# Tiles of every sixteenth token: dilated attention with V as plain rows, ungated w2 and new queue orders

## The chip, the cores and the metric

The kernel runs on one core of a Trainium2 chip. The core has five engines with a queue each: TensorE (PE, with its weight loads as PEld), VectorE (DVE), ScalarE (ACT), GpSimd (POOL) and SyncE (SP), which here issues nearly all DMAs. Each queue is worked through in order, and semaphores tie the queues together. The metric is the device time of one execution in microseconds; lower is better.

## The reference

One transformer block on x of 2048 tokens by 512, with a modulation from c. Attention has 32 heads of 16 and looks, from token s, at the eight tokens s, s - 2, ..., s - 14; tokens before the start are masked.

```python
mod = (_silu(c) @ w_mod).reshape(c.shape[0], 6, 1, -1)      # sa, ca, ga, sb, cb, gb
h = _layernorm(x) * (1 + ca) + sa
x = x + ga * attention(h, A_wqkv, A_wo)                      # W, dil = 8, 2
h = _layernorm(x) * (1 + cb) + sb
x = x + gb * (silu(h @ B_w1) * (h @ B_w3)) @ B_w2            # 512 -> 1792 -> 512
```

## The kernel before

The 2048 tokens are 16 tiles (T) of 128 partitions. Before the change a tile is 128 consecutive tokens, and x, held in SBUF as `x_sb`, is both the input and the running sum.

**Stages.** Modulation: c goes through a tanh on ScalarE (L465), one VectorE operation (L467), a small transpose on TensorE (L470) and a copy by VectorE (L472); then small products with `wm_s` give scale and shift (L504, L487), products with `wm_g` give the gates (L531, L541). LN1 (`ln_stats`): VectorE takes statistics (L555, L556), GpSimd raises to the power -0.5 (L565), VectorE normalizes (L576, and L571 for tile 0). `ln_T` transposes by TensorE (L636, evictions L644 and L651) or by DMA (L621 scales in place) into `h`. Projections Q and K (L691) and V (L711) follow; ScalarE evicts them (L700, L701, L721). V of a tile is stored to a scratch in DRAM.

**Attention of a tile.** VectorE multiplies q with eight shifted copies of K in one operation (`prod`, L742): 8 x 4 x 128 elements a partition. K lies along the free dimension with a pad of 16 columns in front, so a shift by 2w tokens is a start 2w columns earlier. TensorE sums over the head dimension (`red`, L752); for tile 0 a matmul with `before` (L749) adds the mask. Softmax takes VectorE (L764, L769, L794 to L797) and ScalarE (L782); the weights are transposed (L807, L811). `values` loads V back: partition (token, w) of a block holds the rows that this token sees with this w, four DMAs of 128 overlapping runs of 2 KB (two neighbouring rows each). VectorE weights them (L827, in place in `vsh`), TensorE sums over w (L855), ScalarE evicts (L861), a DMA transposes (`ot`), TensorE multiplies with `wo` (L867; its gate `ga` has been multiplied into `wo`, L946), and VectorE adds to `x_sb` and sums the row (L871).

**FFN.** LN2 (`ln_sums`: L586 to L601) runs on GpSimd and ScalarE. For a group of 2 or 4 tiles (`FFN`) and each of 14 blocks of F, `ffn_unit` makes gate and up (L883), the silu on ScalarE (L889) and the product on VectorE (L892). `ffn_w2` sums over F (L921, and L909 in halves for tiles 14 and 15); the gate `gb` has been multiplied into `w2` (L952, four operations), so VectorE only adds `x_sb` (L931) and the result is stored.

**Order.** The program makes a list of 1118 operations. `ORDER` is a written-out list of their numbers that fixes each engine's queue; `SLOTS` gives each rotating buffer. `Program.synchronize` puts a wait where one is needed. `warm` (L518) makes 24 matmuls on a constant, ahead of the first real work.

## Time and profile before

| What | us |
|---|---|
| runs | 238.07, 239.04, 243.02; median 239.04 |
| span of the profiled execution | 237.7 |
| TensorE busy in it | 229.7 |
| VectorE busy | 179.4 |
| ScalarE busy | 138.5 |
| GpSimd busy | 29.2 |

How full the engines are in 40 slices of 5.9 us (each digit is tenths), with the share of the DMA engines:

```profile
PE   7999999999999998999999999999999999999995
...
DVE  5699999999999989999999999682654403434433
ACT  2289577999978744985865594837473405040300
...
DMA  6999999999999999897981693642203000000202
```

VectorE and the DMA engines are full from slice 3 to about slice 25, while attention runs; after that TensorE works through what is left of the FFN. "Busy" of TensorE counts a matmul from its start to the end of its pipeline, so matmuls overlap in it.

### The profile page before, as it was taken

How to read it: one execution, taken by the hardware profiler on the slowest of the kernel's cores; microseconds unless marked ns; L12 is line 12 of the kernel's file. 1: busy time of each engine (PE TensorE's matmuls, PEld its weight loads, DVE VectorE, ACT ScalarE, POOL GpSimd, SP SyncE). 2: the span in 40 equal slices, each digit the busy share in tenths (PEclk: the TensorE clock that was granted, in tenths of full speed). 3: DMA queues.
4: the chain of work that ended last, by engine and by line, in shares of the span. 5: the costliest groups of instructions: out<-in, count | busy, mean ns of one | idle time of the engine just before them, and what ended most of it. 6: DMA issues, size and time to landing. Idle time of an engine off the chain costs nothing.

```text
span 237.7 us, 4535 instructions
## 1 busy us (share of the span) xinstructions
PE 229.7 (97%) x1781; PEld 136.2 (57%) x1806; DVE 179.4 (75%) x279; ACT 138.5 (58%) x267; POOL 29.2 (12%) x66
## 2 busy tenths in 40 slices
PE   7999999999999998999999999999999999999995
PEld 4776454445588674664444444444475457485774
DVE  5699999999999989999999999682654403434433
ACT  2289577999978744985865594837473405040300
POOL 4434100013002000240002520012010000000000
PEclk9999999999999999999999999999999999999999
DMA  6999999999999999897981693642203000000202
GB/s 216 372 337 322 158 237 299 208 269 283 353 200 270 243 249 199 173 260 177 247 234 47 182 234 72 154 132 46 67 19 91 3 0 0 6 19 0 70 0 88
DMA packets 46317, 38.85 MB, mean 163 GB/s; under 512 B 21704, under 2 KB 37080, under 8 KB 46296
## 3 DMA queue, kind: packets, MB, share of 16 engines
q1 hardware_dynamic: 46288, 38.56, 66.9%
q8 instruction: 14, 0.23, 0.4%
q14 instruction: 7, 0.06, 0.1%
q10 hardware_dynamic: 8, 0.00, 0.0%
HBM read 29.62 MB, written 4.21 MB: 142 GB/s over the span
## 4 chain that ended last, share of the span: by engine, by line
PE 74%; DMA 8%; DVE 8%; SPq 4%; ACT 3%; issue 2%; ACTq 0%; DVEq 0%
PE pall L883 38%; PE pall L921 18%; DMA sb_x<-in_A_x_dram 5%; PE pall L867 5%; SPq L124 4%; PE pall L691 4%; DMA sb_vsh<-v_scratch_dram 3%; PE pall L909 3%; PE pall L855 2%; PE pall L752 2%; PE pall L711 2%; DVE sb_vsh L827 2%; DVE sb_pq L742 2%; DVE sb_hh L892 1%; ACT sb_h L621 1%
## 5 line engine op out<-in xcount | busy, mean ns | idle before, releaser
L883 PE MATMUL pall<-sb_h,sb_w 128*128 128x256 bf16 (+1 forms) x664 | 101.9, 307 | 1.8 <-DVE sb_hh L892 0.9
L883 PEld LDWEIGHTS pall<-sb_h,sb_w 128*128 128x128 bf16 x672 | 64.8, 98 | 37.2 <-issue 2.8
L889 ACT ACTIVATE sb_sg<-pall 128x256 bf16<-128x256 f32 (+1 forms) x84 | 35.6, 453 | 54.1 <-PE pall L883 53.0
L892 DVE TENSOR_TENSOR sb_hh<-sb_sg,pall 128x256 bf16<-128x256 bf16 (+1 forms) x84 | 39.9, 505 | 34.8 <-PE pall L883 32.7
L921 PE MATMUL pall<-sb_w,sb_hh 128*128 128x512 bf16 x190 | 44.0, 379 | 0.3
L742 DVE TENSOR_TENSOR sb_pq<-sb_q,sb_kT 128x4096 bf16<-128x4096 bf16 x16 | 36.3, 2282 | 0.0
L921 PEld LDWEIGHTS pall<-sb_w,sb_hh 128*128 128x128 bf16 x196 | 19.0, 98 | 21.6 <-DVE sb_hh L892 0.4
L691 PE MATMUL pall<-sb_h,sb_wqkv 128*128 128x512 bf16 (+1 forms) x154 | 30.2, 335 | 0.5 <-issue 0.2
L827 DVE TENSOR_TENSOR sb_vsh<-sb_vsh,sb_al 128x4096 bf16<-128x4096 bf16 x12 | 27.3, 2287 | 2.1 <-DMA sb_vsh<-v_scratch_dram 2.1
L621 ACT ACTIVATE sb_h<-sb_h,sb_modc 128x512 bf16<-128x512 bf16 (+1 forms) x24 | 16.5, 743 | 10.1 <-DMA sb_h<-sb_xn 10.1
L691 PEld LDWEIGHTS pall<-sb_h,sb_wqkv 128*128 128x128 bf16 x160 | 14.7, 98 | 11.8 <-ACT sb_ac L861 0.4
L931 DVE TENSOR_TENSOR sb_o<-pall,sb_x 128x512 bf16<-128x512 f32 (+1 forms) x18 | 11.1, 625 | 10.5 <-PE pall L921 6.8
L711 PE MATMUL pall<-sb_wqkv,sb_h 128*128 128x512 bf16 x62 | 15.5, 379 | 0.2
L867 PE MATMUL pall<-sb_wo,sb_ot 128*128 128x512 bf16 x61 | 15.3, 379 | 0.3 <-issue 0.2
L586 POOL TENSOR_SCALAR sb_nm<-sb_sx 128x2 f32<-128x2 f32 x8 | 1.7, 218 | 105.2 <-DVE sb_x L871 105.1
L644 ACT ACTIVATE sb_h<-pall,sb_modc 128x256 bf16<-128x256 bf16 (+1 forms) x18 | 9.9, 612 | 7.5 <-DVE sb_modc L509 6.5
L861 ACT ACTIVATE sb_ac<-pall 128x512 bf16<-128x512 f32 x16 | 9.5, 595 | 7.2 <-PE pall L855 7.1
L601 ACT ACTIVATE sb_xn<-sb_x,sb_nb,sb_rs 128x512 bf16<-128x512 bf16 x16 | 12.4, 806 | 0.7 <-POOL sb_nb L599 0.6
L871 DVE SCALAR_TENSOR_TENSOR sb_x<-pall,sb_x 128x512 bf16<-128x512 f32 x16 | 10.9, 686 | 1.5 <-PE pall L867 1.3
L590 ACT ACTIVATE sb_xn<-sb_x,sb_nm 128x512 bf16<-128x512 bf16 x16 | 11.4, 714 | 0.7 <-POOL sb_nm L586 0.7
L721 ACT ACTIVATE sb_v<-pall 128x512 bf16<-128x512 f32 x16 | 9.5, 600 | 2.8 <-PE pall L711 2.8
L555 DVE BATCH_NORM_STATS2 sb_st<-sb_x 128x6 f32<-128x512 bf16 x16 | 10.6, 680 | 0.8 <-DMA sb_x<-in_A_x_dram 0.7
(87 smaller groups left out, 208.3 us busy)
## 6 DMA issues: line engine op xcount, KB each, us to landing
sb_vsh<-v_scratch_dram SPq DMA_DIRECT2D x48, 256.0 KB, 5.5
sb_vshx<-v_scratch_dram SPq DMA_DIRECT2D x16, 256.0 KB, 4.6
sb_w<-in_B_w_dram SPq DMA_DIRECT2D x6, 512.0 KB, 7.9
sb_w<-in_B_w_dram SPq DMA_DIRECT2D x6, 384.0 KB, 5.4
v_scratch_dram<-sb_v SPq DMA_DIRECT2D x16, 128.0 KB, 6.4
out_dram<-sb_o SPq DMA_DIRECT2D x14, 128.0 KB, 1.8
sb_wqkv<-in_A_wqkv_dram SPq DMA_DIRECT2D x6, 256.0 KB, 6.3
sb_x<-in_A_x_dram SPq DMA_DIRECT2D x4, 256.0 KB, 6.4
```

The costliest lines, as they stand in the source:

```text
L590: p.op("act", lambda e, vn=vn, T=T: e.activation(vn.at[:], x_sb[:, T, :], ACT.Square, bias=nm[:, T, :], accum_out=var[:, T, :]), c_act(512 ...
L601: p.op("act", lambda e, vn=vn, T=T: e.activation(vn.at[:], x_sb[:, T, :], ACT.Identity, bias=nb[:, T, :], scale=rs[:, NT + T, :]), c_act(5 ...
L621: return e.activation(vh.at[:, ft, 0:n * P], vh.at[:, ft, 0:n * P], ACT.Identity, bias=modc[:, 8 * which + ft:8 * which + ft + 1], scale=m ...
L691: ins = e.matmul(bank(vp)[:, j * n:(j + 1) * n], wqkv[:, t, col:col + P], vh.at[:, t, 0:n], start=(t == ORDER[0] and j == 0), stop=(t == O ...
L711: ins = e.matmul(bank(vp), vh.at[:, t, tt * P:(tt + 1) * P], wqkv[:, t, 2 * D:3 * D], start=(t == ORDER[0]), stop=(t == ORDER[-1]))
L742: return e.tensor_tensor(vp.at[:], in0, in1, ALU.mult)
L827: return e.tensor_tensor(v_w, v_w, a_w, ALU.mult)
L867: ins = e.matmul(bank(vy), vt.at[:, ft, :], wo[:, ft, :], start=(ft == 0), stop=(ft == KT - 1))
L883: ins = e.matmul(bank(vp)[:, 0:n], wt[:, t, fi * P:(fi + 1) * P], vh.at[:, t, 0:n], start=(t == 0), stop=(t == KT - 1))
L889: p.op("act", lambda e: e.activation(vt.at[:, 0:n], bank(vgp)[:, 0:n], ACT.Silu), c_act(n), k, r=[vgp], w=[vt], table="silu")
L892: p.op("dve", lambda e: e.tensor_tensor(vh_.at[:, 0:n], vt.at[:, 0:n], bank(vup)[:, 0:n], ALU.mult), c_dve(n), k, r=[vt, vup], w=[vh_])
L921: ins = e.matmul(bank(vz), vhh[fi].at[:, tt * P:(tt + 1) * P], w2[:, fi, :], start=(fi == 0), stop=(fi == NF - 1))
```

## The change

**Tokens.** Partition p of tile T holds token 16 p + res(T), where res(T) = 2 (T mod 8) + T // 8. So tiles 0 to 7 hold the even tokens and 8 to 15 the odd ones, and the token two earlier lies in the tile one below, on the same partition; below the lowest tile of a half it is the highest tile, one partition earlier. K needs no pad and `kT` is 2048 columns.

**Products.** `prod` becomes two operations: w = 0 to u (u = T mod 8) with the tiles T to T - u, on all 128 columns, and the other 7 - u with the tiles from the top of the half, on columns 1 to 127. Column 0 of the second part is preset to a large negative number where a buffer needs it, and this takes the place of the `before` mask. A product now needs K of all eight tiles of its half.

**V.** A store writes rows 16 apart. A load is two DMAs of 512 single rows (1 KB), each row of the half once, and waits for the stores of all eight tiles of the half.

**Gate.** `w2` stays as it is. For tiles 0 to 11 ScalarE evicts the sum, VectorE multiplies with `gb` and adds `x_sb`. Ahead of FFN group [12, 13] two VectorE operations put a gated copy of `w2` into the two `vsh` buffers, for tiles 12 to 15.

**LN1.** The first two tiles are normalized as a pair, like the others; the special case for tile 0 goes. The first two pairs, not only the first, have their projections split by quarter of the contraction (`pieces`).

**Orders.** `ORDER` and `SLOTS` are new throughout (1121 operations). Read back into names, the queues begin and run so:

| Queue | before | after |
|---|---|---|
| SP | x 0-1, wms0, wqk0, x 2-3, wqk1, wqk2, wqk3, wv0, wv1, x 4-5, ... | x 2-3, x 0-1, wms0, wqk0, wv0, x 6-7, wqk1, wv1, x 4-5, x 12-15, wqk2, wqk3, ... |
| PE | 7 warm-ups, transpose of c, 17 warm-ups, transposes of tile 0, two of L504, transposes of tile 1, two of L504, K and Q of tiles 0-1 | 18 warm-ups, transpose of c, 4 warm-ups, transposes of tiles 3 and 2, four of L504, Q and K of tiles 2-3, ... (two warm-ups at the very end) |
| VectorE | c, statistics of tile 0, of tile 1, normalize 0, 1 | c, statistics of tiles 2, 3, then 1, 0, normalize 3, 2, ... |
| VectorE, first product | before the statistics of tile 12 and the last four normalizations | after all statistics and normalizations |
| Attention | tiles 0 to 15, by pairs | pairs 0 to 6, then 10, 8, 12 and 14 |
| SP, first V load | after the stores of V of tiles 0 to 2 | after the stores of V of tiles 0 to 7 |

```diff
-    x_view = x2d.rearrange("(t p) d -> p t d", p=P)
+    NU = NT // 2
+    x_view = x2d.rearrange("(p u e) d -> p e u d", p=P, e=2)
+    out_view = out2d.rearrange("(p u e) d -> p e u d", p=P, e=2)
+
+    def res(T):
+        return 2 * (T % NU) + T // NU
...
-    kT = sb([P, KT, PAD + S], bf, "kT")
+    kT = sb([P, KT, S], bf, "kT")
...
-        vh.pieces = [Val(f"h_{ft}") for ft in range(KT)] if not which and not gi else None
+        vh.pieces = [Val(f"h_{ft}") for ft in range(KT)] if not which and gi < 2 else None
...
-        p.dma(v_dram[PAD + T * P:PAD + (T + 1) * P, :], lambda: vt.at[:], k, (128, 1024), r=[vt], w=[vd], cost=400, store=True)
+        p.dma(bass.AP(v_dram, (PAD + res(T)) * D, [[NT * D, P], [1, D]]), lambda: vt.at[:], k, (128, 1024), r=[vt], w=[vd], cost=400, store=True)
...
-                in0 = bass.AP(vq[cch].at, tt * P, [[KT * 512, P], [0, W], [512, KT], [1, P]])
-                in1 = bass.AP(kT, PAD + T * P, [[KT * (PAD + S), P], [-DIL, W], [PAD + S, KT], [1, P]])
-                return e.tensor_tensor(vp.at[:], in0, in1, ALU.mult)
...
+                row, n = W * KT * P, W - 1 - u
+                q = lambda m, c: bass.AP(vq[cch].at, tt * P + c, [[KT * 512, P], [0, m], [512, KT], [1, P - c]])
+                k = lambda t, m, c: bass.AP(kT, t * P, [[KT * S, P], [-P, m], [S, KT], [1, P - c]])
+                o = lambda w, m, c: bass.AP(vp.at, w * KT * P + c, [[row, P], [KT * P, m], [P, KT], [1, P - c]])
+                if preset.get(vp.slot, W) > u + 1:
+                    e.memset(bass.AP(vp.at, (u + 1) * KT * P, [[row, P], [P, n * KT], [1, 1]]), BEFORE)
+                preset[vp.slot] = u + 1
+                ins = e.tensor_tensor(o(0, u + 1, 0), q(u + 1, 0), k(T, u + 1, 0), ALU.mult)
+                if n:
+                    ins = e.tensor_tensor(o(u + 1, n, 1), q(n, 1), k(top, n, 1), ALU.mult)
+                return ins
...
-        for q in range(4):
-            p.dma(lambda q=q: vv.at[:, 2 * q:2 * q + 2, :],
-                  bass.AP(v_dram, (PAD + T * P + 32 * q) * D, [[2 * D, 16], [-DIL * D, W], [1, 2 * D]]), ("vl", T), (128, 2048),
-                  r=[vv_dram[T]] + ([vv_dram[T - 1]] if T else [vvpad]), part=[vv], group=loads, cost=640, again=True)
+        c = T // NU * NU
+        for b in range(0, 8, 4):
+            p.dma(lambda b=b: vv.at[:, b:b + 4, :],
+                  bass.AP(v_dram, (PAD + res(T) - DIL * (W - 1) + 256 * b) * D, [[2 * D, P], [256 * D, 4], [1, D]]), ("vl", T), (512, 1024),
+                  r=[vv_dram[t] for t in range(c, c + NU)] + [vvpad], part=[vv], group=loads, cost=470)
...
+        vo = Val("o", opool)
+        k = ("zo", T)
+        p.op("act", lambda e: e.activation(vo.at[:], bank(vz), ACT.Copy), c_act(512), k, r=[vz], w=[vo])
+        o = p.op("dve", lambda e: e.tensor_tensor(vo.at[:], vo.at[:], gb_bc[:], ALU.mult), 340, k, r=[vg[1]], w=[vo], lock=True)
+        p.op("dve", lambda e: e.tensor_tensor(vo.at[:], vo.at[:], x_sb[:, T, :], ALU.add), 340, k, r=[vx[T]], w=[vo], lead=o, lock=True)
...
-        vns = [v for pr in ([[T] for T in Ts] if gi == 0 else pairs(Ts)) for v in ln_stats(pr)]
+        vns = [v for pr in pairs(Ts) for v in ln_stats(pr)]
...
+        if Ts[-1] == NT - 3:
+            for i, (a, b) in enumerate(((0, 8), (8, NF))):
+                p.op("dve", lambda e, i=i, a=a, b=b: e.tensor_tensor(w2v[i].at[:, 0:b - a, :], w2[:, a:b, :],
+                                                                     bass.AP(gb_bc, 0, [[D, P], [0, b - a], [1, D]]), ALU.mult),
+                     48 + 274 * (b - a), ("mod", 7 + i), r=vw2 + [vg[1]], w=[w2v[i]], lock=True)
```

105 lines of the change are left out of this document (38 added, 67 removed), and 132 rows, old and new, of tables (ORDER, SLOTS).

## The prediction

> **What bounds the kernel now.** I read the page first: how full each engine is, then the chain of work that ended last.
>
> ```profile
> span 237.7 us, 4535 instructions
> ...
> PE 229.7 (97%) x1781; PEld 136.2 (57%) x1806; DVE 179.4 (75%) x279; ACT 138.5 (58%) x267; POOL 29.2 (12%) x66
> ...
> PE 74%; DMA 8%; DVE 8%; SPq 4%; ACT 3%; issue 2%; ACTq 0%; DVEq 0%
> ```
>
> TensorE is busy for 97% of the span and makes 74% of the chain. Busy can hide gaps, so the next question is pace. Two lines of the chain in order of time (start, length, what) give it:
>
> ```profile
> 188.98 6.04 PE pall L921 x28
> ...
> 207.82 6.11 PE pall L883 x56
> ```
>
> That is 6.04 / 28 = 216 ns for a matmul of 512 columns and 6.11 / 56 = 109 ns for one of 256: a steady stream. Where is TensorE not streaming? The busy time in windows (window, length, PE, weight loads, DVE, ACT, POOL, clock, DMA share, GB/s), and then the timeline of TensorE (start, length):
>
> ```profile
> 10.00:235.00 225.00, 221.62 (x1704) 130.46 (x1727) 172.17 (x252) 136.34 (x264) 24.76 (x46) 1.00 0.67 160
> ```
> ```profile
> 1.24 1.68 PE L518 MATMUL pall<-sb_ones 128*128 128x256 bf16 x7 [1.24 <-DVE sb_ones L375]
> 3.35 0.18 PE L470 MATMUL pall<-sb_ident,sb_c4s 4*128 4x4 bf16 x1 [0.43 <-DVE sb_c4s L467]
> 3.46 3.14 PE L518 MATMUL pall<-sb_ones 128*128 128x256 bf16 x17
> 6.53 0.40 PE L636 MATMUL pall<-sb_ident,sb_xn 128*128 128x128 bf16 x4
> ...
> 7.63 0.54 PE L504 MATMUL pall<-sb_csT_bf,sb_wm_s 128*128 128x1 bf16 x16
> 8.19 0.61 PE L691 MATMUL pall<-sb_h,sb_wqkv 128*128 128x256 bf16 x4
> ...
> 229.73 5.29 PE L909 MATMUL pall<-sb_w,sb_hh 128*128 128x256 bf16 x47
> ```
>
> The projections start at 8.19, the last matmul ends at 235.02, and between 10 and 235 TensorE idles 225.00 - 221.62 = 3.4 us in all. So the span is 8.19 (head) + 223.4 (streaming) + 3.4 (waits) + 2.7 (last result to the end) = 237.7 us. The change keeps every large matmul, so the 223.4 stays. It can win at most the 3.4, and it can lose in the head and in new waits. The profiled span is 1.3 us under the median of the runs, 239.04; I add that 1.3 at the end.
>
> **The head.** In the new queue of TensorE the transpose of c (L470) stands behind eighteen warm-ups; before it stood behind seven. Seven took 1.68 us, the last of them 0.38, so one starts every (1.68 - 0.38) / 6 = 0.217 us: 18 x 0.217 = 3.9, and the transpose starts at 1.24 + 3.9 = 5.15 in place of 3.35. On VectorE the copy of its result stands ahead of the first LN statistics, in both orders:
>
> ```profile
> 3.57 0.16 DVE L472 TENSOR_SCALAR sb_csT_bf<-pall 128x4 bf16<-128x4 bf16 x1 [0.27 <-PE pall L470]
> 3.71 0.69 DVE L555 BATCH_NORM_STATS2 sb_st<-sb_x 128x6 f32<-128x512 bf16 x1
> ...
> 5.73 0.74 DVE L571 SCALAR_TENSOR_TENSOR sb_xn<-sb_x,sb_mv,sb_rs 128x512 bf16<-128x512 bf16 x1
> 6.93 0.41 DVE L576 TENSOR_SCALAR sb_xn<-sb_x,sb_mv,sb_rs 128x512 bf16<-128x512 bf16 x1 [0.46 <-POOL sb_rs L565]
> ...
> 8.43 1.27 DVE L555 BATCH_NORM_STATS2 sb_st<-sb_x 128x6 f32<-128x512 bf16 x2
> ...
> 11.02 0.74 DVE L576 TENSOR_SCALAR sb_xn<-sb_x,sb_mv,sb_rs 128x512 bf16<-128x512 bf16 x2 [1.05 <-POOL sb_rs L565]
> ```
>
> So the statistics move from 3.71 to 3.71 + 1.8 = 5.5. A pair then goes as the pair at 8.43 did: 11.02 - 8.43 = 2.6 to the first normalized tile and 0.74 for two, so 8.85; the other pair's two statistics fill the 1.05 us wait. From the last normalized tile to the first projection it was 8.19 - 7.34 = 0.85; all 32 small products of L504 now lie in that stretch and not 16 of them, which adds about 0.25. Start: 9.95, **+1.75 us**. The joint pair saves nothing that shows: L571 at 0.74 becomes a 0.41, inside this sum. Swapping loads (x of tiles 2 and 3 first, `wms0` third) moves `wms0` back by one issue and 256 KB, but its use moves from 6.76 to 9.1. Lower bound +1.0, if the warm-ups ran at the pace of the seventeen, (3.14 - 0.38) / 16 = 0.173.
>
> **Attention waits for eight tiles.** Keys and V rows of one tile now come from all eight tiles of its half. The first product, which began at 22.89 with keys of four tiles, needs 10.4 us of projections for four tiles (2 x 32 x 0.109 + 2 x 8 x 0.216 for each two), K of four more (16 x 0.216 = 3.5), one V (0.9) and 2.5 of transposes and gates ahead of it: 9.95 + 17.3 = 27.2, with its eviction about 28. VectorE has 18.6 us of LN work queued before it in the new order, from 5.5 to 24.1, so it waits a little. TensorE does not: it has the other projections. The first product meets its reduction where the queue of TensorE has it (32.6).
>
> The V rows are closer. V of the last of the eight tiles leaves TensorE at 9.95 + 21.7 = 31.7, is evicted by 32.5, and three stores are issued by 34. Then the load of tile 0 is queued on SP behind the landing of those stores, and everything behind it on SP waits too.
>
> ```profile
> sb_vsh<-v_scratch_dram SPq DMA_DIRECT2D x48, 256.0 KB, 5.5
> ...
> v_scratch_dram<-sb_v SPq DMA_DIRECT2D x16, 128.0 KB, 6.4
> ```
> ```profile
> DMA to landing us min/median/max: 1.9/6.4/7.9
> ```
> ```profile
> 70.00:80.00 10.00, 9.89 (x95) 1.00 1.02 248
> ```
> ```profile
> 5.00:6.00 1.00, 1.00 (x7) 1.00 1.04 399
> ```
>
> A store lands in 1.9 to 7.9 us (second answer: the stores of V); I take 4, because the loads of the start are through by 34. Two issues (1.2) and a landing (5.5) make 44.7 for tile 0. TensorE's own sum reaches its weighted V rows (L855) at 45.0, and they need another 2.3 of VectorE: a wait of 2.0, and the next tile's about 0.6 more, against 20.00 - 19.73 = 0.3 us idle between 40 and 60 before. **+2.2 us**, bounds 0.5 (stores in 1.9) and 5 (stores in 6.4). Behind it the output projection, LN2 and the first FFN tile follow with no spare.
>
> Once running, V is lighter. The old overlapping rows ran at 248 GB/s with the DMA engines full (third fence), the start's loads at 399 (fourth): 1 MB a tile in 2.6 us rather than 4.2 if plain rows go at that rate. SP issues two loads a tile, not four, some 16 x 2 x 0.6 = 19 us of issuing. What this can return:
>
> ```profile
> 80.00:100.00 20.00, 18.72 (x167) 1.00 0.99 211
> 40.00:60.00 20.00, 19.73 (x172) 1.00 1.10 262
> ```
> ```profile
> DVE sb_vsh L827 <- DMA sb_vsh<-v_scratch_dram: 2.1, 3, 1.0
> ```
>
> The worst stretch, 80 to 100, idles 1.3 us. I take **-0.8** (0 to -2).
>
> **VectorE and ScalarE work.**
>
> ```profile
> L742 DVE TENSOR_TENSOR sb_pq<-sb_q,sb_kT 128x4096 bf16<-128x4096 bf16 x16 | 36.3, 2282 | 0.0
> L892 DVE TENSOR_TENSOR sb_hh<-sb_sg,pall 128x256 bf16<-128x256 bf16 x56 | 21.8, 417 | 25.2 <-PE pall L883 24.9
> L892 DVE TENSOR_TENSOR sb_hh<-sb_sg,pall 128x512 bf16<-128x512 bf16 x28 | 18.5, 682 | 9.6 <-PE pall L883 7.8 <-ACT sb_sg L889 1.7
> L946 DVE TENSOR_TENSOR sb_wo<-sb_wo,sb_ga_bc 128x2048 bf16<-128x2048 bf16 x1 | 1.2, 1217 | 0.0
> L952 DVE TENSOR_TENSOR sb_w<-sb_w,sb_gb_bc 128x2048 bf16<-128x2048 bf16 x2 | 2.4, 1216 | 0.0
> L952 DVE TENSOR_TENSOR sb_w<-sb_w,sb_gb_bc 128x1536 bf16<-128x1536 bf16 x2 | 1.8, 952 | 0.0
> L931 DVE TENSOR_TENSOR sb_o<-pall,sb_x 128x512 bf16<-128x512 f32 x14 | 9.5, 682 | 6.8 <-PE pall L921 6.8
> L392 DVE MEMSET sb_ind<- 128x32 uint32 x1 | 0.1, 85 | 0.0
> L861 ACT ACTIVATE sb_ac<-pall 128x512 bf16<-128x512 f32 x16 | 9.5, 595 | 7.2 <-PE pall L855 7.1
> L889 ACT ACT_TABLE_LOAD x5 | 6.4, 1283 | 0.1
> L749 PE MATMUL pall<-sb_before,sb_ones 128*32 128x256 bf16 x1 | 0.3, 283 | 0.0
> ```
> ```profile
> 190.00:200.00 10.00, 9.95 (x67) 6.39 (x66) 1.77 (x4) 2.88 (x8) 0.00 (x0) 1.00 0.00 0
> ```
>
> bf16 from SBUF costs (2282 - 1217) / 2048 = 0.52 ns an element plus 0.15 us. Splitting 14 of 16 products adds about 0.1 us each and some 0.085 us memsets: +2 us on VectorE. Scaling w2 (2.4 + 1.8 = 4.2) leaves its full stretch and returns late, where VectorE has 8 of 10 us free (window 190 to 200). Twelve tiles swap a PSUM add of 0.68 for two SBUF operations of 0.42, and ScalarE gets 12 x 0.6 = 7.1 us, plus two table loads (1.3 each) by the new order of its exponentials; ScalarE has 100 us free. On TensorE's path: 0. If that cover went, 12 x (0.6 + 0.84 - 0.68) = 9 us would show. The `before` mask and its matmul are worth 0.3 us at most.
>
> **Sum.** 9.95 + 223.4 + (3.4 + 2.2 - 0.8) + 2.7 = 240.85 for the span; with 1.3, **242.1 us**. With the bounds of its terms: 239.5 to 245.
>
> **Rivals.**
>
> *The odd start.* The second product writes from column 1, reads q from column 1, 127 elements a row: a start of 2 bytes. No row here has one. If it goes one element at a time, the price is the slope of L892, (682 - 417) / 256 = 1.035 ns in place of 0.52. Each half has 7 + 6 + ... + 0 = 28 such rows of 4 x 127 elements, so 2 x 28 x 508 x 0.515 = 14.7 us more on VectorE. It decides once it exceeds VectorE's lead: adding up each engine's new queue at the durations of these rows, VectorE weights tile 5 at 75 to 78 and TensorE wants it at 83, a lead of 5. Then 14.7 - 5 = 9.7: 252 us (245 to 257). [...] Every bf16 product from SBUF that the trace does show, 1536 to 4096 elements, runs at the faster pace, and none starts odd: 10%.
>
> *The clock falls.* With 22 warm-ups done by about 5.9 and the first normalized tile at 8.5, TensorE idles 2.6 us, then does small work until 9.95.
>
> ```profile
> 230.00:240.00 10.00, 5.02 (x47) 4.26 (x44) 2.30 (x5) 0.00 (x0) 0.00 (x0) 0.91 0.17 52
> ```
>
> The granted clock drops to 0.91 of the last window, at half rate 0.18 of it: 1.8 us before 240, about 3 us after the last matmul. A pause of 2.6 us is just short. If it falls, the warm-up's pace (0.217 for 0.109) holds for some 3 us and costs 1.3 to 2.5: 243.4 to 244.6. [...] 12%.
>
> *V stays slow.* Stores in 6.4 us, and rows no cheaper than before, because every load still touches all rows of a half: 5 in place of 2.2 at the start and again about 2 at tile 8's loads: 246.5 to 248. 10%.
>
> *The order absorbs it.* V lands early, lighter queues leave 1.5 us of waits: 9.95 + 223.4 + 1.5 + 2.7 + 1.3 = 238.9, (237.3 to 239.5). For it: SP and DMA relief. 20%. Below 234.3 the head would have to be shorter than before too: 3%.
>
> **Numbers.** Forecast 45%, the others 10, 12, 10, 20 and 3. A result within 2% (about what this kernel's runs can tell) lies between 234.3 and 243.8: most of the forecast (0.39), the absorbing order (0.20) and half the clock (0.05): 0.64. Slower: 0.33. Faster: 0.03. Range 237.3 to 248: it leaves out the odd start and the very fast ends. The forecast's own range is 239.5 to 245.
>
> **What would show it.** First statistics near 5.5 and first projection near 10 (head); idle before the first weighted V rows and its releaser a DMA (V); the mean of the split product's second part, at 0.52 or 1.035 ns an element; granted clock and matmul pitch between 9 and 13; PE idle from 80 to 100. The prediction is wrong if the projections start by 8.5, or if waits between 10 and the last matmul sum to over 8 us.

## The result, and the profile after

| | before | after |
|---|---|---|
| median of 4 runs, us | 239.11 | 249.32 |
| lowest and highest, us | 238.07, 243.02 | 248.79, 249.47 |
| span of the profiled execution, us | 237.7 | 247.5 |

The change makes the kernel slower by a factor of 1.0429 (95% interval 1.0401 to 1.0457). 249.3 us lies above the forecast of 242.1 and above the end of its range, 248.0.

The page of the changed kernel (busy time and share of the span; then the shares of the chain that ended last):

```profile
span 247.5 us, 4536 instructions
...
PE 233.9 (95%) x1780; PEld 137.7 (56%) x1805; DVE 180.9 (73%) x309; ACT 145.6 (59%) x279; POOL 23.1 (9%) x63
...
PE 77%; DMA 11%; ACT 4%; DVE 3%; issue 2%; SPq 1%; POOL 1%; ACTq 0%
```

VectorE has 1.5 us more work than before and ScalarE 7.1, so no engine has become much heavier, and yet the span is 9.8 us longer. The windows of the changed kernel say where (window, length, then busy time of PE, weight loads, DVE, ACT and POOL, granted clock, DMA share, GB/s):

```profile
9.00:16.00 7.00, 6.23 (x60) 4.32 (x61) 5.56 (x21) 2.04 (x4) 1.58 (x3) 0.51 1.08 366
...
20.00:60.00 40.00, 37.29 (x302) 19.81 (x306) 28.62 (x45) 30.93 (x55) 2.73 (x6) 0.96 0.89 232
...
43.00:47.00 4.00, 4.00 (x12) 1.50 (x11) 2.89 (x3) 2.73 (x6) 0.00 (x0) 0.57 1.06 358
11.00:244.80 233.80, 226.99 (x1717) 133.16 (x1742) 175.50 (x291) 144.05 (x277) 19.97 (x46) 0.98 0.55 154
```

and of the kernel before:

```profile
20.00:60.00 40.00, 39.51 (x344) 20.13 (x351) 39.70 (x48) 33.56 (x64) 5.44 (x9) 1.00 1.16 254
...
8.20:235.00 226.80, 223.26 (x1716) 131.65 (x1741) 173.94 (x259) 136.91 (x265) 24.76 (x46) 1.00 0.68 161
```

- From the first projection to the last matmul TensorE idles 233.80 - 226.99 = 6.8 us, where it idled 226.80 - 223.26 = 3.5: **+3.3**.
- The granted clock is 0.51 from 9 to 16 and 0.57 from 43 to 47; the trace's clock records have half rate from 9.01 to 15.84 and from 43.14 to 46.56. Projections run at half rate from 11.08 to 15.84 and work of the middle for 3.41 us, which costs (4.76 + 3.41) / 2 = **4.1**.
- The first projection starts at 11.08 and not at 8.19: **+2.9**.

These make 10.3 for a difference of 9.8; the 0.5 left over is not traced. Each of the two traces lacks 25 matmul records (x1780 here for 1805 weight loads), and some 2 us of each idle time are such gaps of under 0.17 us: the traces of e4 and e5, which lack no record, have one between them. The difference of 3.3 is hardly touched by that.

TensorE's timeline of the head and of the middle (start, length, work, and in brackets the idle time before and what ended it):

```profile
1.24 4.02 PE L518 MATMUL pall<-sb_ones 128*128 128x256 bf16 x18 [1.24 <-DVE sb_ones L379]
5.19 0.18 PE L470 MATMUL pall<-sb_ident,sb_c4s 4*128 4x4 bf16 x1
...
8.61 0.90 PE L630 MATMUL pall<-sb_ident,sb_xn 128*128 128x128 bf16 x8 [2.58 <-DVE sb_xn L570]
9.91 1.01 PE L504 MATMUL pall<-sb_csT_bf,sb_wm_s 128*128 128x1 bf16 x32 [0.40 <-DMA sb_wm_s<-in_w_mod_dram]
11.08 1.01 PE L685 MATMUL pall<-sb_h,sb_wqkv 128*128 128x256 bf16 x4 [0.15 <-DVE sb_modc L509]
...
42.84 1.64 PE L685 MATMUL pall<-sb_h,sb_wqkv 128*128 128x512 bf16 x4 [2.21 <-ACT sb_v L715]
...
52.63 0.62 PE L839 MATMUL pall<-sb_vsh,sb_ind 128*32 128x512 bf16 x8
...
66.08 0.29 PE L630 MATMUL pall<-sb_ident,sb_xn 128*128 128x128 bf16 x2 [0.84 <-ACT sb_xn L595]
```

In the head the transpose of c is at 5.19 (forecast 5.15). After the warm-ups there is a pause of 2.6 us, the clock falls, and then the small products of the modulation wait for `wms0`, whose DMA is the releaser in the fourth line.

The longest stall behind the head is at 42.84. The timelines of ScalarE and of VectorE around it:

```profile
30.92 0.60 ACT L695 ACTIVATE sb_kT<-pall 128x512 bf16<-128x512 f32 x1 [0.27 <-PE pall L685]
...
40.28 0.81 ACT L615 ACTIVATE sb_h<-sb_h,sb_modc 128x512 bf16<-128x512 bf16 x1 [3.09 <-DMA sb_h<-sb_xn]
```
```profile
31.72 0.43 DVE L742 TENSOR_TENSOR sb_pq<-sb_q,sb_kT 128x512 bf16<-128x512 bf16 x1
...
48.33 2.29 DVE L829 TENSOR_TENSOR sb_vsh<-sb_vsh,sb_al 128x4096 bf16<-128x4096 bf16 x1 [2.44 <-DMA sb_vsh<-v_scratch_dram]
```

and VectorE in the kernel before:

```profile
22.89 4.48 DVE L742 TENSOR_TENSOR sb_pq<-sb_q,sb_kT 128x4096 bf16<-128x4096 bf16 x2
...
36.86 4.49 DVE L827 TENSOR_TENSOR sb_vsh<-sb_vsh,sb_al 128x4096 bf16<-128x4096 bf16 x2
```

The projections at 42.84 were released by ScalarE's eviction of a V (L715), and ScalarE, in order, had waited 3.1 us for a DMA transpose until 40.28. Eight microseconds later VectorE waits 2.4 us for V. Attention as a whole is late: the first product starts at 31.72 (before 22.89), the first weighting of V at 48.33 (before 36.86), the first FFN matmul at 69.67 (before 61.7). The windows from 20 to 60 show it: VectorE was busy 39.70 of 40 us before, and is now at 28.62, waiting for its first inputs, while its total work is nearly the same.

### The profile page after: what moved, and what is told of

Same layout as the page of the kernel before. It is cut to its first block, busy times and chain, and to the rows that moved or that the text cites. A ratio compares the mean times of both kernels' runs of the same rounds, so it can differ in the third digit from the quotient of the medians.

```text
span 247.5 us, 4536 instructions
## 1 busy us (share of the span) xinstructions
PE 233.9 (95%) x1780; PEld 137.7 (56%) x1805; DVE 180.9 (73%) x309; ACT 145.6 (59%) x279; POOL 23.1 (9%) x63
## 4 chain that ended last, share of the span: by engine, by line
PE 77%; DMA 11%; ACT 4%; DVE 3%; issue 2%; SPq 1%; POOL 1%; ACTq 0%
PE pall L867 35%; PE pall L908 14%; PE pall L685 9%; PE pall L851 5%; PE pall L705 5%; DMA sb_vsh<-v_scratch_dram 4%; DMA sb_wm_s<-in_w_mod_dram 3%; PE pall L839 3%; PE pall L896 2%; PE pall L753 2%; ACT sb_h L615 1%; DMA sb_ot<-sb_ac 1%; DMA sb_h<-sb_xn 1%; SPq L124 1%; DMA v_scratch_dram<-sb_v 1%
## 5 line engine op out<-in xcount | busy, mean ns | idle before, releaser
L873 ACT ACTIVATE sb_sg<-pall 128x256 bf16<-128x256 f32 (+1 forms) x84 | 34.8, 458 | 33.1 <-PE pall L867 29.0
L908 PE MATMUL pall<-sb_w,sb_hh 128*128 128x512 bf16 x165 | 37.4, 379 | 0.4 <-issue 0.2
L685 PE MATMUL pall<-sb_h,sb_wqkv 128*128 128x512 bf16 (+1 forms) x157 | 32.9, 349 | 2.9 <-ACT sb_v L715 2.2
L829 DVE TENSOR_TENSOR sb_vsh<-sb_vsh,sb_al 128x4096 bf16<-128x4096 bf16 x11 | 25.2, 2287 | 6.6 <-DMA sb_vsh<-v_scratch_dram 3.9
L908 PEld LDWEIGHTS pall<-sb_w,sb_hh 128*128 128x128 bf16 x168 | 16.2, 98 | 18.9 <-issue 0.6
L742 DVE TENSOR_TENSOR sb_pq<-sb_q,sb_kT 128x512 bf16<-128x512 bf16 (+7 forms) x16 | 21.6, 1350 | 0.0
L705 PE MATMUL pall<-sb_wqkv,sb_h 128*128 128x512 bf16 x60 | 17.2, 414 | 0.3 <-ACT sb_q L694 0.2
L744 DVE TENSOR_TENSOR sb_pq<-sb_q,sb_kT 128x3556 bf16<-128x3556 bf16 (+6 forms) x14 | 17.1, 1223 | 0.0
L638 ACT ACTIVATE sb_h<-pall,sb_modc 128x256 bf16<-128x256 bf16 (+1 forms) x16 | 8.8, 622 | 10.3 <-DVE sb_modc L509 8.1
L829 DVE TENSOR_TENSOR sb_vshx<-sb_vshx,sb_al 128x4096 bf16<-128x4096 bf16 x5 | 11.4, 2289 | 1.1 <-DMA sb_vshx<-v_scratch_dram 0.9
L715 ACT ACTIVATE sb_v<-pall 128x512 bf16<-128x512 f32 x16 | 9.5, 604 | 3.6 <-PE pall L705 3.5
```

Source lines behind the costliest of these rows:

```text
L685: ins = e.matmul(bank(vp)[:, j * n:(j + 1) * n], wqkv[:, t, col:col + P], vh.at[:, t, 0:n], start=(t == ORDER[0] and j == 0), stop=(t == O ...
L705: ins = e.matmul(bank(vp), vh.at[:, t, tt * P:(tt + 1) * P], wqkv[:, t, 2 * D:3 * D], start=(t == ORDER[0]), stop=(t == ORDER[-1]))
L742: ins = e.tensor_tensor(o(0, u + 1, 0), q(u + 1, 0), k(T, u + 1, 0), ALU.mult)
L744: ins = e.tensor_tensor(o(u + 1, n, 1), q(n, 1), k(top, n, 1), ALU.mult)
L829: return e.tensor_tensor(v_w, v_w, a_w, ALU.mult)
L873: p.op("act", lambda e: e.activation(vt.at[:, 0:n], bank(vgp)[:, 0:n], ACT.Silu), c_act(n), k, r=[vgp], w=[vt], table="silu")
```

## The experiments

All were run beside the kernel before on the same chip; ratios are to it. "Releaser" is what ended a wait.

| run | median (lowest to highest), us | ratio (95% interval) |
|---|---|---|
| e1 transpose of c behind 7 warm-ups | 250.6 (249.4 to 252.2) | 1.049 (1.043 to 1.055) |
| e2 the same, `wms0` second | 249.6 (248.0 to 250.2) | 1.043 (1.037 to 1.049) |
| e3 22 more warm-ups | 249.9 (248.1 to 252.4) | 1.040 (1.034 to 1.047) |
| e4 before, transpose behind 18 | 241.8 (241.3 to 242.2) | 1.011 (1.007 to 1.015) |
| e5 whole head | 248.0 (246.2 to 248.4) | 1.033 (1.026 to 1.039) |
| e6 V's transfers ahead | 249.5 (247.7 to 252.0) | 1.038 (1.029 to 1.046) |
| e7 e5 and e6 | 248.1 (246.0 to 249.1) | 1.033 (1.024 to 1.041) |
| e8 V loads wait for no store | 250.3 (248.9 to 251.6) | 1.044 (1.036 to 1.051) |
| e9 e7, V projected earlier | 247.5 (245.0 to 248.7) | 1.032 (1.023 to 1.041) |
| e10 e7, first V loads at 30 us | 248.9 (247.9 to 249.3) | 1.038 (1.033 to 1.043) |
| e11 gating 2 columns wide | 249.4 (248.9 to 250.0) | 1.041 (1.036 to 1.046) |
| e12 after, all queues re-ordered | 252.7 (251.8 to 253.8) | 1.056 (1.050 to 1.061) |
| e13 before, all queues re-ordered | 252.1 (250.7 to 253.2) | 1.052 (1.046 to 1.059) |
| e14 e9, first product earlier | 247.6 (245.9 to 248.4) | 1.032 (1.025 to 1.039) |
| e15 e14, GpSimd kept free | 245.1 (244.9 to 248.3) | 1.029 (1.021 to 1.037) |
| e16 e15, two queue moves | 250.9 (250.3 to 251.7) | 1.050 (1.044 to 1.057) |
| e17 e15, the queue laid out anew | 245.3 (244.9 to 245.5) | 1.025 (1.015 to 1.035) |

Runs of one kernel scatter by 1 to 4 us, so differences between neighbouring rows of 1 us are not told apart; what a run is used for below is mostly a wait that its profile shows or no longer shows.

### The head: e1 to e5

```diff
 queue of TensorE (e1)
   7 warm-ups
+  transpose of c
   11 warm-ups
-  transpose of c
```


> The changed kernel with the transpose of c behind 7 warm-up matmuls instead of 18, as in the kernel before; nothing else. Theory A (the statistics that wait for it set the head): the first statistics start at about 3.9 instead of 5.49 us, everything behind them up to the first projection moves by the same 1.5 us (11.08 to about 9.6), and the time falls from 249.3 to about 247.8. Theory B (the modulation weights set the head: they landed at 9.86, third behind both pairs of x): statistics and transposes go early, the first modulation product stays at 9.9, the first projection at 10.6 to 11.1, and the time stays within 0.5 of 249.3.

```diff
 queue of SP (e2, on top of e1)
   x 2-3
+  wms0
   x 0-1
-  wms0
```


> As the run before, and the modulation weights issued second, between the two pairs of x, as in the kernel before. Theory B: the weights land at about 7, the first projection starts at 8.2 to 9.0, TensorE is never idle for 2.5 us and its clock stays at 1.0 from 5.7 on; the time falls by 2.5 (head) plus about 2.4 (clock), to 244.0 to 245.0. Theory A alone would have it no better than the run before. If the slow clock is not what cost 2.4 us, the time falls by the head alone, to about 246.8.

```diff
-            return e.matmul(bank(vw)[:, 0:256], ones[:, 0:P], ones[:], start=True, stop=True)
+            for _ in range(23 if i == 18 else 1):
+                ins = e.matmul(bank(vw)[:, 0:256], ones[:, 0:P], ones[:], start=True, stop=True)
+            return ins
```


> The changed kernel with 22 more warm-up matmuls in the last warm-up step, which fill TensorE's 2.6 idle microseconds before the first transposes; every other start in the head stays (first projection about 11). Theory C (the idle stretch lowered the clock and the lowered clock is paid for): granted 1.0 from 5.6 to about 43, and the time falls by 2.4 to about 246.9. Rival (in those microseconds TensorE waits for weights anyway): the clock is whole and the time falls by less than 0.7.

e4 is the kernel before with the transpose of c moved behind eighteen warm-ups:

```diff
   7 warm-ups
-  transpose of c
   11 warm-ups
+  transpose of c
   6 warm-ups
```


> The kernel before with its transpose of c behind 18 warm-up matmuls instead of 7, nothing else. By the prediction's first term this costs 1.75 us (first statistics 3.71 to about 5.5, first projection 8.19 to 9.95) and the time is 240.8. If the idle stretch that it opens behind the warm-ups (6.0 to about 8.1) lowers the clock as it did in the changed kernel, 2 to 2.5 us come on top, 242.8 to 243.3. If the other waits of the head swallow it, 239 to 239.5.

e5 is e2 with VectorE's and TensorE's queues of the head put in the order in which data lands:

```diff
 queue of VectorE
-  statistics of tiles 1, 0; normalize 1, 0
   columns of the modulation (L509), first evictions (L645)
+  statistics of tiles 1, 0; normalize 1, 0
 queue of TensorE: transposes of tiles 1, 0 behind the first V projections
```


> The run before this one (transpose of c behind 7 warm-ups, modulation weights second) had its statistics early, but VectorE, which works in order, stood 2.18 us at the first pair's statistics, whose x now landed at 7.5, with the second pair's normalizations behind them; the first projection stayed at 11.2. Here the first pair's statistics and normalizations are also put behind the modulation columns and the second pair's evictions on VectorE, and its transposes behind the second pair's first products on TensorE. Theory D (VectorE's order was all that held the head back): first projection at 8.2 to 9.2, no half clock, 2.5 us of head and 2.4 us of clock gained against the changed kernel, 244.0 to 245.0. Rival E (the V chain of 36 to 50 us does not start earlier with the head, so that TensorE waits there instead): first projection as in theory D, stalls at 42 and 52 us grow by as much, time 247 to 249.

TensorE in e1, e2, e4 and e5, one line of the head each (e2 and e5 have two):

```profile
10.16 1.01 PE L504 MATMUL pall<-sb_csT_bf,sb_wm_s 128*128 128x1 bf16 x32 [2.47 <-DMA sb_wm_s<-in_w_mod_dram]
```
```profile
9.20 1.03 PE L630 MATMUL pall<-sb_ident,sb_xn 128*128 128x128 bf16 x8 [2.29 <-DVE sb_xn L570]
...
11.22 1.01 PE L685 MATMUL pall<-sb_h,sb_wqkv 128*128 128x256 bf16 x4 [0.15 <-DVE sb_modc L509]
```
```profile
8.18 0.51 PE L636 MATMUL pall<-sb_ident,sb_xn 128*128 128x128 bf16 x4 [2.16 <-DVE sb_xn L571]
```
```profile
8.64 0.60 PE L685 MATMUL pall<-sb_h,sb_wqkv 128*128 128x256 bf16 x4 [0.19 <-DVE sb_modc L509]
...
12.03 0.72 PE L630 MATMUL pall<-sb_ident,sb_xn 128*128 128x128 bf16 x8 [1.63 <-DVE sb_xn L570]
```

The place of the transpose alone gains nothing (e1): the small products then wait for `wms0` until 10.16, 2.5 us. With `wms0` second, it lands at 6.72 in place of 9.87, and the wait goes to the normalized tiles (e2: 9.20), because VectorE, in order, stands 2.2 us at the statistics of tiles whose x is not there yet. The head of e2 runs at half rate: its trace holds no clock record and so shows 1.00, but the four matmuls at 11.22 take 1.01 us, and the same four take 0.60 in e5. Only with all three queues mended (e5) do the projections start at 8.64, and then the next pair is awaited at 12.03. In the kernel before, the same move of the transpose costs 1.1%, 2.7 us (e4), with half clock from 8.33 to 15.16: the forecast had 1.75 for it. e3 keeps the clock whole until 53 us and gains nothing that shows: TensorE then waits 2.1 us at 41.18 and 2.2 at 52.48 instead. The time that the clock no longer lost came back as waits for the chain behind.

### V: e6 to e10

e6 (and e7, which is e5 and e6 together) moves two weight loads on SP behind V of tile 1, and on ScalarE an exponential and a V eviction ahead of two modulations that wait for DMA transposes:

```diff
 queue of SP
-  wo1, w1_0
   V of tiles 0, 1
+  wo1, w1_0
 queue of ScalarE
+  EXP of tiles 0, 1; eviction of V 14
   two modulations (L615) of tiles 12 to 15
-  EXP of tiles 0, 1; eviction of V 14
```


> The changed kernel with its head as it is; on SyncE's queue the loads of part of wo and of the first piece of w1 go behind the first four loads of V instead of ahead of the last three stores of V (1.3 us), and on ScalarE the first softmax's exponential and the eviction of V of tile 14 go ahead of two modulations that wait for a DMA transpose (3.09 us at 37.2 in the changed kernel). Theory F (these two orders make the stall at 42.8 and with it the second half clock): the 2.4 us stall falls under 0.8, the second clock window is gone (1.7 us), the first AV product starts at about 46.5 instead of 48.3; time 245.5 to 247. Rival (TensorE only catches up and waits at the next tile's V or at the second normalization): 248 to 249.5.

> Both of the two runs above together. If head and V chain are separate costs, their gains add: 240.5 to 242.5, within 2% of the kernel before. If they are one chain, no better than the better of the two, 244 to 247.

e8 loads the V tiles from the modulation weights, so that no load waits for a store:

```diff
-                  bass.AP(v_dram, (PAD + res(T) - DIL * (W - 1) + 256 * b) * D, [[2 * D, P], [256 * D, 4], [1, D]]), ("vl", T), (512, 1024),
-                  r=[vv_dram[t] for t in range(c, c + NU)] + [vvpad], part=[vv], group=loads, cost=470)
+                  bass.AP(w_mod.tensor, w_mod.offset + (PAD + res(T) - DIL * (W - 1) + 256 * b) * D, [[2 * D, P], [256 * D, 4], [1, D]]), ("vl", T), (512, 1024),
+                  part=[vv], group=loads, cost=470)
```


> The changed kernel, with the loads of V for every tile reading as many bytes in the same pattern from the modulation weights' memory and so waiting for no store of V; the place of each load on its queue is kept, and the output is not the reference's. Theory G (waiting for the stores of eight tiles before the first load is the cost): loads are issued about 2.4 us earlier at 38.5 and at the second half's start, the stalls at 42.8 to 52 and at 60 to 72 shrink; time 246 to 247.5. Rival (the loads' place behind other work on SyncE and their own 8 us at full DMA share): time within 0.7 of 249.3.

e9 projects, evicts and stores V of tiles 6, 7 and 4 ahead of other work of their group, with the weight loads behind the V loads; e10 is e7 with the loads for tiles 0 and 1 alone taken from the modulation weights, at 30 us.

> The run with head and V orders together (248.1), and the last three tiles' V (4, 6 and 7) taken forward everywhere: projected before two of the four query products of their group, evicted before the modulations of tiles 12 to 15, stored before the last DMA transpose; the loads of the first two tiles' V directly behind, and weights that nobody needs before 54 us (part of w1, of wo, of the second modulation) behind those loads. Theory H (what the head's repair ran into is the chain V store, V load, AV product, first FFN tile, and its length is set by queue orders): loads issued at about 35 instead of 37.0, first AV product at 42.5 (then bound by its softmax) instead of 43.8 and the second at 44.8 instead of 47.1, the stalls at 49.5, 54.8 and 63 us (1.9, 0.9, 1.1) shrink by 2 in sum, 246. Rival I (the DMA engines: 2 MB of V for two tiles land 7 to 10 us after issue whatever is ahead): second AV product still 10 us behind the first load's issue, time 247.5 to 248.5.

> The run with head and V orders together, and V of the first two tiles loaded from the modulation weights' memory, so that it waits for no store, and issued ahead of the last transposes, at about 29; the output is not the reference's. It shows what is left of the middle when V is simply there. Theory H: AV products directly behind their softmax (42.5 and 44.8), time 245.5 to 246.5, as the run beside it or better by at most 1. If the softmax chain and the second normalization, not V, hold the first FFN tile: the stall at 49.5 goes but those at 54.8 to 66.6 grow by as much, 247.5 to 248.5.

TensorE in e6, VectorE in e10, then VectorE and TensorE in e9:

```profile
53.10 0.81 PE L839 MATMUL pall<-sb_vsh,sb_ind 128*32 128x512 bf16 x8 [2.33 <-DVE sb_vsh L829]
```
```profile
47.37 4.49 DVE L829 TENSOR_TENSOR sb_vsh<-sb_vsh,sb_al 128x4096 bf16<-128x4096 bf16 x2 [3.23 <-ACT sb_al L812]
```
```profile
30.05 0.41 DVE L570 TENSOR_SCALAR sb_xn<-sb_x,sb_mv,sb_rs 128x512 bf16<-128x512 bf16 x1 [2.21 <-DMA sb_h<-sb_xn]
30.41 0.43 DVE L742 TENSOR_TENSOR sb_pq<-sb_q,sb_kT 128x512 bf16<-128x512 bf16 x1
...
43.71 4.49 DVE L829 TENSOR_TENSOR sb_vsh<-sb_vsh,sb_al 128x4096 bf16<-128x4096 bf16 x2
```
```profile
55.01 1.90 PE L851 MATMUL pall<-sb_wo,sb_ot 128*128 128x512 bf16 x8 [1.94 <-DMA sb_ot<-sb_ac]
```

e6 removes the stall of 42.84 and meets one of 2.3 at the weighted V (53.10). The wait for eight stores is not what holds V: SyncE stood 0.3 us for it in the changed kernel, and without it (e8) the loads are still issued at 41.45 (after: 41.22), by their place on SP. With V there early (e10), VectorE waits 3.2 us for the softmax weights instead. In e9 both first weightings run back to back at 43.71, 4.6 us earlier than in the changed kernel, and TensorE waits 1.9 at the output projection. Each repair holds where it was made and the time hardly follows.

### Gating: e11

```diff
-        o = p.op("dve", lambda e: e.tensor_tensor(vo.at[:], vo.at[:], gb_bc[:], ALU.mult), 340, k, r=[vg[1]], w=[vo], lock=True)
+        o = p.op("dve", lambda e: e.tensor_tensor(vo.at[:, 0:2], vo.at[:, 0:2], gb_bc[:, 0:2], ALU.mult), 340, k, r=[vg[1]], w=[vo], lock=True)
```


> The changed kernel with the gating of finished tiles reduced from 512 columns to 2 (the multiplication by the gate is left out on twelve tiles, so the output is not the reference's). By the prediction the twelve multiplications lie beside TensorE's work and cost nothing: 249.3 within 0.7. If VectorE's 12 times about 0.3 us were on the path, 246 to 247.

249.4 against 249.3 us: the gating multiplication of twelve tiles costs nothing that shows.

### Order or layout: e12 and e13

Both kernels were given queues from the same search, which places operations by the durations that the traces show; e12 also has ten more warm-ups.

```diff
-ORDER = [ 15, 14, 1, 4, 0, 5, 17, 73, 63, 52, 64, 62,
+ORDER = [ 0, 77, 56, 17, 52, 72, 16, 70, 1, 63, 53, 79,
```


> The changed kernel with the same operations (and ten warm-up matmuls more), but all queues in another order and other buffer numbers: an order searched anew with the durations that the traces show, in which the first normalizations, the modulation weights, the V stores and loads and the first products no longer stand behind each other's waits. Theory K (the loss is in the new queue orders, not in the new layout of tiles, the split products, or the gating): 236 to 242, the 7 to 10 us are gone. Theory L (keys and V of eight tiles ahead of the first product use up the work that TensorE has for the time of the first softmax, whatever the order): not below 244.


```diff
-ORDER = [ 8, 9, 10, 0, 20, 21, 22, 3, 4, 1, 2, 16,
+ORDER = [ 1, 3, 20, 8, 55, 56, 16, 0, 77, 17, 74, 65,
```


> The kernel before with all queues in another order and other buffer numbers, searched in the same way and with the same effort as the run beside it; nothing else changed. It says what the search itself is worth: if it brings the kernel before to 236 to 240 (no change), what the run beside it gains over 249.3 is the repair of that kernel's orders; if it makes the kernel before slower by several us, the search is poor and the run beside it is an upper bound for the layout.

TensorE in e12 and in e13:

```profile
65.16 0.40 PE L632 MATMUL pall<-sb_ident,sb_xn 128*128 128x128 bf16 x2 [3.61 <-ACT sb_xn L597]
```
```profile
62.02 0.61 PE L636 MATMUL pall<-sb_ident,sb_xn 128*128 128x128 bf16 x8 [2.31 <-ACT sb_xn L601]
```

By e12 alone theory L would stand, for 252.7 us is not below 244. But the search makes both kernels slower than they were, and about equally slow, 252.7 and 252.1, with a stall at LN2 in each. So the old layout loses 13 us to its order alone, and orders from one poor search do not tell the two layouts apart. That allows the order as the cause and does not show it; only a search that finds an order as good as that of before could.

### The chain taken apart: e14 to e17

e14 is e9 with the first product ahead of the normalization of tile 11, which waited for a buffer (the third fence of V, 30.05):

```diff
 queue of VectorE
-  normalize 11
   first product
+  normalize 11
```


> The run with V taken forward (247.5), and one more edit: the first product goes ahead of the normalization of tile 11 on VectorE (and that tile's DMA transpose behind it on SyncE). In that run the keys were evicted at 28.9, but the product started at 30.41, behind this normalization, which stood 2.21 us for a buffer that a DMA transpose still read. Theory H: first product at 29.0, the stall at 35.2 (1.4) falls to about 0, 246 or a little more. Rival: the same microsecond comes back at the output projection (2.1 at 55.0) and the second normalization (1.5 at 63 to 67), 247 to 248.

The first product now starts at 29.21 and a wait of 1.2 us at 35.15 is gone; the output projection waits 2.25 in place of 1.94, and the time is 247.6.

e15 makes the fifth product wait for the last small GpSimd operation of the first LN2 pair:

```diff
         p.op("pool", lambda e: e.tensor_tensor(nb[:, i:i + n, 0], nm[:, i:i + n, 0], rsn, ALU.mult), 210, k, r=[vr, vnm], w=[vb], lead=o)
+        nbs[i] = p.ops[-1]
...
+    prods[4].deps[nbs[0]] = True
```


> e14_products_ahead with one wait added: the fifth key product (tile 4) on VectorE starts only when GpSimd has finished the third small operation of the first LN2 pair (nb). Theory that GpSimd's small operation is held until a long VectorE product ends: the power (L591) takes about 0.7 us in place of 1.97, the normalized tiles begin about 1.2 us earlier after the squares, the two waits of TensorE in front of the first FFN tile (1.0 and 0.5 us) shrink by about 1 us together, and the time is 246.5 against 247.6. Rival (the power takes as long as it takes, whatever VectorE does): 1.9 us again, the waits unchanged, 247.6 or a little more for the later product.

The timelines of VectorE and GpSimd in e14, and of GpSimd, VectorE and TensorE in e15:

```profile
59.92 1.48 DVE L742 TENSOR_TENSOR sb_pq<-sb_q,sb_kT 128x2560 bf16<-128x2560 bf16 x1
...
60.00 1.97 POOL L591 TENSOR_TENSOR sb_rs<-sb_rs,sb_cst 128x2 f32<-128x2 f32 x1
```
```profile
59.07 0.71 POOL L591 TENSOR_TENSOR sb_rs<-sb_rs,sb_cst 128x2 f32<-128x2 f32 x1
...
60.09 1.49 DVE L744 TENSOR_TENSOR sb_pq<-sb_q,sb_kT 128x2560 bf16<-128x2560 bf16 x1 [1.02 <-POOL sb_nb L593]
...
61.29 0.28 PE L631 MATMUL pall<-sb_ident,sb_xn 128*128 128x128 bf16 x2
```

Two numbers a partition take 1.97 us beside the product and 0.71 without it: 59.92 + 1.48 is 61.40, and 61.97 is 0.57 later. TensorE's wait at the LN2 transposes, which stood at 0.84 to 0.99 us in the changed kernel and in e3, e6 to e10 and e14, is gone (61.29, no bracket). Three of four runs lie at 245, one at 248.3; the ratio's interval overlaps e14's, and e14's profiled run had half rate from 9.00 to 12.41 where e15's had none, so the profile shows the mechanism and the time only suggests its size.

e16 and e17 change the queue of SP:

```diff
 e16, on top of e15
-  w1_0, w1_3, w3_3
   first two transposes of the attention output
+  w1_0, w1_3, w3_3
...
-  V 10 (second half)
   last two transposes of the third FFN group
+  V 10 (second half)
```


> e15 with two moves on the SP queue: three FFN weight loads (w1_0, w1_3, w3_3) behind the first two transposes of the attention output, and one V load of the second half (VL10.1) behind the last transpose of the third FFN tile. Theory that the later waits come from transfers that land strictly in the order of issue: the wait ahead of the output projection (2.4 us at 55 in e14) falls under 0.7, the wait for the third FFN tile (2.3 us at 120) falls under 0.5, and the time is 243.5 to 244.5. Rival (the next late thing of the same chain takes the time back, as in the earlier repairs): 246 to 247. Second rival (the loads that are moved back become late): a wait at the first FFN weights or the V rows of tiles 8 to 11, 247 to 249.


```diff
 e17, on top of e15
   w1_0
-  w1_3, w3_3
   first two transposes of the attention output
-  V 3 (first half), w1_1, w3_0, V 3 (second half)
+  w1_1, V 3, w1_3
   V 2
+  w3_3, w3_0
...
-  V 8 (first half)
   transposes of the third FFN group, V 11, V 10
+  V 8 (first half)
```


> e15 with the SP queue laid out by the landings that e15 and e16 show, without e16's two moves: the first two transposes of the attention output stand ahead of all but one FFN weight load (w1_0), V of tiles 3 and 2 is ahead of w3_3 and w3_0, which are used later, and in the second half the V load that is used last (VL8.0) stands behind the transposes of the third FFN tile and behind V of tiles 10 and 11. Theory that transfers landing in the order of issue hold the remaining waits: at the output projection 2.0 falls to about 0.8, at the third FFN tile 1.5 falls under 0.5, no wait of over 1 us at the V rows (e16 had 2.5, 2.9 and 1.9 there); 242.5 to 243.5 us. Rival (the chain hands the time on): 244.5 to 246, with a new wait of over 1.5 us behind one of the two places.

TensorE in e14, in e16 and in e17, with e17's window from the first projection to the last matmul:

```profile
55.15 1.90 PE L851 MATMUL pall<-sb_wo,sb_ot 128*128 128x512 bf16 x8 [2.25 <-DMA sb_ot<-sb_ac]
...
119.63 5.35 PE L867 MATMUL pall<-sb_h,sb_w 128*128 128x512 bf16 x24 [2.16 <-ACT sb_h L615]
```
```profile
67.41 0.96 PE L841 MATMUL pall<-sb_vsh,sb_ind 128*32 128x512 bf16 x8 [2.24 <-DVE sb_vsh L831]
70.73 1.04 PE L841 MATMUL pall<-sb_vsh,sb_ind 128*32 128x512 bf16 x8 [2.36 <-DVE sb_vsh L831]
```
```profile
67.25 0.61 PE L841 MATMUL pall<-sb_vsh,sb_ind 128*32 128x512 bf16 x8 [1.57 <-DVE sb_vsh L831]
...
8.90:240.80 231.90, 223.48 (x1715) 131.40 (x1741) 176.78 (x294) 143.58 (x277) 19.40 (x47) 1.00 0.59 157
```

The two waits of e14, which stand at 1.80 and 1.37 in e15, are gone in e16 and in e17, so transposes behind loads did hold them. In e16 the price is V of tiles 3 and 2, which land at 65.0 and 68.4 (e15: 60.7 and 65.4), TensorE pauses twice for over 2 us there, and the clock halves from 67.54 to 74.37: 250.9 us, more than any range that had been named for it. In e17 the pause is 1.6 us, the clock stays whole, and the time is e15's within the scatter, its four runs close together: the rival of e17, that the chain hands the time on, is what came. TensorE still idles 231.90 - 223.48 = 8.4 us at full clock, against 3.5 before (this trace, too, lacks 25 records).

No version beat the kernel before: the best, e17, lies 2.5% above it (1.5 to 3.5). The times of e1, e2, e4, e7, e8, e10, e15 and e16 lie outside every figure that was named for them, mostly above it: what a repair is worth could not be told from the wait that it removes.

## Why the prediction was wrong, point by point

**Right.** The statistics of LN start at 5.49 (5.5). The streaming is unchanged (226.99 - 4.1 = 222.9 us against 223.3). ScalarE's twelve evictions take 7.0 us (7.1) and two table loads came (1.28 us each), as in the working; that its whole work grew by just 7.1 is because other groups shrank. From 80 to 100 us, where the working looked for relief of 0.8, TensorE idles 0.2 us and not 1.3. V did not stay slow by its stores: the last three landed in 2.2 to 2.7 us, where that rival had 6.4. The odd start (of q and of the output; K starts even) runs at the fast pace, so that rival fell; the rows of L744 with 508 and with 3556 elements give (2023 - 420) / 3048 = 0.526 ns an element, and 508 take no longer than 512 that start even (L920). These are groups by form of the changed kernel (busy, mean ns of one):

```profile
L920 DVE TENSOR_TENSOR sb_o<-sb_o,sb_gb_bc 128x512 bf16<-128x512 bf16 x12 | 5.0, 420 | 2.2 <-ACT sb_o L919 2.2
...
L744 DVE TENSOR_TENSOR sb_pq<-sb_q,sb_kT 128x3556 bf16<-128x3556 bf16 x2 | 4.0, 2023 | 0.0
...
L744 DVE TENSOR_TENSOR sb_pq<-sb_q,sb_kT 128x508 bf16<-128x508 bf16 x2 | 0.8, 420 | 0.0
```

That is shown for this one operation alone. Gating costs nothing (e11), and no wait of TensorE in the trace is put down to the moved scaling of `w2`.

**The sum of the miss.** 249.3 - 242.1 = 7.2 us: 1.1 in the head, 4.1 of slow clock and 2.0 of waits.

**Head, forecast +1.75, came +2.9.** The first pair is normalized by 8.87, as worked out (8.85). The step that failed is the stretch from there to the first projection, taken as 1.1 us; it took 2.2. Of the 1.1 us missed, 0.4 is the wait for `wms0` (the fourth line of TensorE's head): "`wms0` moves back by one issue and 256 KB, but its use moves from 6.76 to 9.1" took the load to be in time. It landed at 9.87, 5.1 us after the load ahead of it; issued second, it lands at 6.71 (before) and 6.72 (e2), about 3 us after. From 4 to 6.5 us the DMA engines moved 198 GB/s where they moved 401 before; why the transfer is slower in third place stays open. The rest is the stretch itself, which was sized too short: with the weights in time and a whole clock it takes 1.4 us in e5 (7.21 to 8.64), and the transposes at the falling clock took 0.90 us in place of e5's 0.72.

**Clock, given 12%, came.** "A pause of 2.6 us is just short" was wrong. The pause was 2.58 us, and the clock fell at 9.01, 0.4 us after it; in e4 it was 2.16 and the clock fell at 8.33. Length alone does not decide: in e14 half rate from 9.00 to 12.41 follows a pause of no more than 0.87 us (and forty small matmuls), while the pause of 2.25 us at 55.15 of the same trace passes without a fall. The pieces of one clock in the changed kernel's trace, without the last, which runs to its end, are 3.41, 6.83, 27.31, 3.41 and 201.39 us long, within 0.03 us 1, 2, 8, 1 and 59 times 3.413. So there the rate changed only on a step of that length, and it is the author's estimate from these five pieces that the place of a pause on that step counts and not its length alone; no run moved a pause along it. That the slow pace holds for some 3 us was an estimate too, which no trace of the kernel before shows; half rate lasted 6.83 and 3.41 us in the changed kernel. Yet the clock is a symptom as much as a cause: two of e3's runs kept it whole throughout and took 248.1 and 249.2 us.

**Waits after 10 us, forecast 4.8 in all, came 6.8 of idle time and, beside it, 4.1 of slow clock.** The idle time alone stays under the bound of 8 us that the prediction set itself; with the slow clock it is 10.9. (Of the 3.4 us that it read as waits in the kernel before, some 2 are records that the trace lacks.)

The path of V came as worked out, but 3.5 us late, by the head (1.1) and the half rate up to 15.84 (2.4): V of the last of the eight tiles left TensorE at 35.20 (31.7), and tile 0's rows had landed at 48.31 (44.7). The wait of 2.0 that the working had for TensorE at these rows did not come: it reached them at 52.63 without a pause (45.0), because it had stood 2.2 us at 42.84 and lost 1.7 to the half rate behind that. What VectorE waits there, 2.4 us, is another quantity. Two sentences of the prediction failed:
- "VectorE has 18.6 us of LN work queued before it ..., so it waits a little. TensorE does not: it has the other projections." The first product came at 31.72 (forecast 28). Its last keys left ScalarE at 31.52, late by the same 3.5 us, so VectorE's queue did not hold it here; it comes next, for in e9 the keys are out at 28.9 and the product stands till 30.41 behind a normalization that waits 2.2 us. TensorE's projections did not cover the delay: at 42.84 the next one waits for an eviction by ScalarE, which had waited 3.1 us for a DMA transpose. And VectorE, which had no free time from 20 to 60 us before, idles 11 us there now.
- "Behind it the output projection, LN2 and the first FFN tile follow with no spare", at no price. The price is there: each of softmax, V, output projection, LN2 and FFN tile is a hand-over through another engine or a DMA, and TensorE's projections are used up by then. e5, e6, e9, e14, e15 and e17 each shortened one hand-over, and a later wait took most of the gain.

The repairs together give 1.025 against 1.043: some 4 of 10 us came back (the intervals do not meet), by the times mostly with the whole head (e5) and with GpSimd kept free (e15), though neither step is clear of the scatter by itself. Of the 6.0 us that e17's span (243.7) is over that of before, 0.7 is its head (first projection at 8.91) and 8.4 - 3.5 = 4.9 are waits. Whether another order would win these back, or whether needing K and V of all eight tiles before the first attention tile sets a floor, is open.

## What to carry to other kernels

When a change makes the first piece of a stage need all of the inputs and not a part, price every hand-over of the chain behind it, to the point where the busiest engine next depends on it; that engine's other work hides the delay only until it runs out. A wait that is repaired by hand moves to the next link as long as the whole chain is late, so look at when each stage begins in the two traces before looking at single stalls. In a queue that lands in order, as SP's did in the changed kernel (136 of 136), a small transfer on the critical chain belongs ahead of the bulk loads that were issued before it; e16 shows the other side, that the loads moved back can become the next late thing.
